# An inverse DFT in even and odd frequencies, q sums at full width, and cheaper tables in an attention-and-gate kernel

## The chip, the cores and the metric

The kernel runs on one core of a Trainium2 chip. The metric is the device time of one execution in microseconds. Most executions agree within about 1%. Each run has a state: "slow" if it lies over 1.5% above the fastest of the same kernel.

A core has a matmul engine (TensorE, "PE" in the profile), an elementwise engine (VectorE, "DVE"), an engine for copies and activations (ScalarE, "ACT"), GpSimd ("POOL"), a queue for transfers (SyncE, "SP"), and 16 DMA engines that move the data.

## The reference, cut to what matters

Two stages run one after the other, for 8 batches of 576 positions.

```python
def _attn_ref(q, k, v):                      # (8, 8, 576, 64) each
    m = 32
    q_lm = q.reshape(B, H, m, S // m, D).mean(axis=3)      # landmarks: sums of 18 rows
    k_lm = k.reshape(B, H, m, S // m, D).mean(axis=3)
    A, Bm, C = sm(q, k_lm), sm(q_lm, k_lm), sm(q_lm, k)    # three softmaxes
    Z = ...                                                # pseudo-inverse of Bm
    for _ in range(6):
        Z = 2 * Z - Z @ Bm @ Z                             # Newton steps
    return A @ Z @ C @ v

def _moe_ref(x, w_proj, filter_fft, w_out):  # x: the attention's output, (8, 576, 512)
    x1, x2, x3 = split(x @ w_proj)
    X2 = np.fft.rfft(x2, n=S, axis=1)
    H = np.fft.rfft(filter_fft, n=S, axis=0)
    y = x1 * np.fft.irfft(X2 * H, n=S, axis=1) * x3        # S = 576
    return y @ w_out
```

## The kernel before: the parts that the argument touches

The program is a prologue (load, landmarks and attention of batch 0, sine and cosine tables, spectrum of the filter) and then eight "gates". Gate `b` is woven step by step with the attention of batch `b + 1`, so that TensorE has work of one while the other waits.

The q sums add rows in groups of 18 with matmuls against a 0/1 matrix. A matmul takes a pair of a head's six columns. The middle pair belongs half to landmarks 0 to 15 and half to landmarks 16 to 31, so it is done as two matmuls that write 64 output rows each:

```python
def pool_q(h0):
    pl2 = st["pl"].rearrange("p (t h l) -> p t h l", t=2, h=H)
    for h in range(h0, h0 + 4):
        for x in (0, 2):
            mm(pl2[:, 1, h, :], qn[:, h, 2 * x:2 * x + 2, :]..., poolq[:, x // 2, :],
               start=(x == 0), stop=False)
        for par in range(2):
            mm(pl2[64 * par:64 * par + 64, 1, h, :], qn[:, h, 2 + par, :],
               poolq[:, par, :], start=False, stop=True)
```

The inverse DFT makes both halves of the 576 positions (`e` = 0, 1) from all frequencies, and VectorE multiplies the result in PSUM with the gates:

```python
def inverse(j):
    pi = wtile()
    for f in range(2):
        for t in range(2):
            for e in range(2):
                mm(pi[:, e, 0:HS], st["Y"][:, f, t, P * j:P * j + P],
                   INV[:, 2 * f + t, HS * e:HS * e + HS], ...)
    o = slice(64 * (j // 2), 64 * (j // 2) + 64)
    for e in range(2):
        mm(pi[:, e, 0:HS], st["YE"][o, ...], INV[o, 4, HS * e:HS * e + HS], ...)
    nc.vector.tensor_tensor(st["y"][:, j, :]..., pi[:, :, 0:HS], st.pop(f"gt{j}"), op=ALU.mult)
```

The filter is prepared in these lines. The tag of a tile names the ring of (here two) buffers that it is taken from; the tables' scratch tile `u` also has the tag "Y":

```python
def trig(dst, t, np_, shape):
    u = big.tile([np_] + shape, F32, tag="Y", name="u")
    ...                                     # three VectorE instructions and one Sin per table part
def filter_spectrum():
    fs = big.tile([R, 2, 3, Dm], F16, tag="Y", name="fs")
    nc.vector.tensor_tensor(fs[:, 0], filt[:, 0], filt[:, 1], op=ALU.add)
    nc.vector.tensor_tensor(fs[:, 1], filt[:, 0], filt[:, 1], op=ALU.subtract)
    ...
```

At the end of each gate `output(n)` multiplies the `y` of all four `j` with `wout`.

The softmax here doesn't subtract the row's maximum and nothing guards it: scores larger than these inputs give would overflow.

## Time and profile before

| | before |
|---|---|
| median of 3 runs | 293.62 us (293.33 to 296.63) |
| span of the profiled run, granted clock | 291.9 us, 0.972 |
| first AE matmul of the eight gates (first forward transform) | 52.7, 84.6, 114.2, ... 263.9 us |
| first spectral product on VectorE (`T`) of the eight gates | 61.1, 92.4, 122.0, ... 269.2 us |
| period of an undisturbed gate | 29.56 us |
| of it: first `T` to last `y`, last `y` to next `T` | 18.2 and 11.4 us |

The last four rows are read from the timeline; two of the seven periods were about 1 us longer at a lower granted clock.

The page of the kernel before: busy time by engine with its share of the span, then busy tenths of TensorE and VectorE in 40 slices of 7.3 us.

```profile
PE 249.2 (85%) x3642; PEld 149.3 (51%) x3642; DVE 166.6 (57%) x365; ACT 145.9 (50%) x247; POOL 31.9 (11%) x69
PE   0776108979999999999999999999989998999990
DVE  1279994066834684368417761867186718682830
```

After the prologue (the first seven slices) TensorE is full, and nothing else is. The 85% is an average of a prologue with holes and a steady state with hardly any. A window in the steady state shows that; columns: window, its length, then busy time and instructions of PE, weight loads, DVE, ACT and POOL, granted clock, DMA share, GB/s.

```profile
220.00:250.00 30.00, 29.20 (x467) 17.74 (x465) 17.53 (x36) 17.09 (x30) 0.00 (x0) 1.00 0.15 41
```

TensorE is busy for 29.20 of 30 us. The chain of waits through one period (92.4 to 122 us), shares by engine and line, agrees: 79% of it is matmuls.

```profile
by line: PE w L77 55.5%; PE s L77 23.7%; DVE T L580 8.3%; ACT X L578 3.5%; ACT G L569 3.1%; ACT eC L301 2.0%; DVE Y L582 2.0%; ACT lmp L211 2.0%; PE s L393 1.7%; DVE Bn L235 0.8%; issue 0.7%; DVE rB L232 0.4%; DVE rB L233 0.3%
```

The groups that the change touches; columns: line, engine, operation, out<-in, count, then busy us and mean ns of one, then the idle time of the engine just before them and what ended it.

```profile
L77 PE MATMUL w<-INV,Y 128*128 128x288 f16 x256 | 37.7, 287 | 0.2 <-ACT x_5153 L614 0.2
L631 DVE TENSOR_TENSOR y<-w,gt 128x576 bf16<-128x576 f32 x32 | 24.1, 752 | 11.0 <-PE w L77 11.0
L77 PE MATMUL w<-wout,y 128*128 128x512 bf16 x128 | 30.2, 380 | 0.0
```

The 287 ns are the time from a matmul's start to its modelled end. What a matmul costs in a full queue is the distance to the next start, and that is read from TensorE's timeline (start, duration of the group, what):

```profile
205.45 0.45 PE L77 MATMUL s<-poolk,kn 96*128 96x32 bf16 x12
...
206.97 1.20 PE L77 MATMUL s<-poolq,qn 96*128 96x32 bf16 x16
...
226.52 1.16 PE L77 MATMUL w<-INV,Y 128*128 128x288 f16 x8
227.61 0.41 PE L77 MATMUL w<-INV,YE 64*128 64x288 f16 x2
227.95 0.20 PE L77 MATMUL s<-RZ,identh 128*128 128x64 f16 x1
```

One inverse goes from 226.52 to 227.95: 1.43 us. Sixteen q sums take 1.13 us to the next start where twelve k sums of the same size take about 0.3: the q sums alternate between 128 and 64 output rows.

The prologue in TensorE's timeline; the bracket is the idle time before the group and what ended it.

```profile
45.09 6.59 PE L77 MATMUL w<-fs,F 96*128 96x512 f16 x18 [14.54 <-DVE fs L501]
...
52.69 0.90 PE L77 MATMUL w<-F,AE 96*128 96x288 f16 x6
```

VectorE's timeline just before that, in the same columns:

```profile
43.72 0.45 DVE L408 TENSOR_TENSOR u<-u,t 128x288 f32<-128x288 f32 x1
44.08 0.95 DVE L501 TENSOR_TENSOR fs<-filt 96x1536 f16<-96x1536 bf16 x1
```

TensorE waits 14.54 us for the filter sums `fs`, and `fs` runs only when the last table's `u` is done.

### The profile page before, as it was taken

To read this page: it belongs to the slowest core of one execution; us is meant where nothing else is said; L and a number is where in the kernel's file an instruction comes from. 1 tells how busy PE (TensorE), PEld (TensorE's weight loads), DVE (VectorE), ACT (ScalarE), POOL (GpSimd) and SP (SyncE) were. 2 spreads that over 40 slices of the span, in tenths; PEclk is the share of its full clock that TensorE was granted. 3 is DMA by queue.
4 is the path that set the end of the run, shared out by engine and by line. 5 is a ranking of instruction groups with operands and counts; after the bars stand their busy time and mean duration, and the time that the engine had idled before them with its cause. 6 is when DMAs were issued, how large, how long until landed. Compare 5 with 4: busy or idle time off the path is not lost.

```text
span 291.9 us, 8299 instructions
## 1 busy us (share of the span) xinstructions
PE 249.2 (85%) x3642; PEld 149.3 (51%) x3642; DVE 166.6 (57%) x365; ACT 145.9 (50%) x247; POOL 31.9 (11%) x69
## 2 busy tenths in 40 slices
PE   0776108979999999999999999999989998999990
PEld 0653102636655565556555656565656565654550
DVE  1279994066834684368417761867186718682830
ACT  1036132776258724872467435852685169518421
POOL 8871000200111010101020102001000000000000
PEclk9999999978999999999979998999999999999998
DMA  7999999996689958995899489939500050005005
GB/s 93 201 209 199 198 178 180 175 158 83 91 165 183 135 90 147 191 147 86 147 183 141 77 138 188 153 59 142 164 3 2 2 162 2 2 2 163 2 0 162
DMA packets 66420, 35.07 MB, mean 120 GB/s; under 512 B 46736, under 2 KB 62096, under 8 KB 66384
## 3 DMA queue, kind: packets, MB, share of 16 engines
q0 software_dynamic: 27280, 16.84, 42.5%
q1 hardware_dynamic: 39104, 17.70, 29.8%
q8 instruction: 28, 0.46, 0.6%
q14 instruction: 8, 0.07, 0.1%
HBM read 33.69 MB, written 9.44 MB: 148 GB/s over the span
## 4 chain that ended last, share of the span: by engine, by line
PE 73%; DVE 11%; ACT 9%; DMA 3%; issue 2%; POOL 0%; ACTq 0%; POOLq 0%
PE w L77 50%; PE s L77 20%; DMA qn<-in_q_dram 3%; DVE T L580 3%; ACT X L578 2%; ACT eC L301 2%; ACT G L569 2%; PE s L190 1%; DVE Y L582 1%; PE s L393 1%; DVE u L408 1%; ACT lmp L211 1%; DVE u L405 1%; DVE t L439 1%; DVE Bn L235 1%
## 5 line engine op out<-in xcount | busy, mean ns | idle before, releaser
L77 PE MATMUL w<-AT,G 128*128 128x288 f16 x256 | 43.4, 292 | 0.8 <-ACT x_5179 L614 0.2
L77 PE MATMUL w<-INV,Y 128*128 128x288 f16 x256 | 37.7, 287 | 0.2 <-ACT x_5153 L614 0.2
L631 DVE TENSOR_TENSOR y<-w,gt 128x576 bf16<-128x576 f32 x32 | 24.1, 752 | 11.0 <-PE w L77 11.0
L77 PE MATMUL w<-wout,y 128*128 128x512 bf16 x128 | 30.2, 380 | 0.0
L77 PEld LDWEIGHTS <-G 128*128 128x128 bf16 x256 | 21.5, 99 | 13.9 <-issue 7.6
L215 DVE TENSOR_SCALAR lm<-s 128x512 bf16<-128x512 f32 x8 | 5.5, 690 | 38.8 <-PE s L77 38.8
L77 PEld LDWEIGHTS <-Y 128*128 128x128 bf16 x256 | 22.0, 98 | 8.5 <-DVE Y L582 1.4
L580 DVE TENSOR_TENSOR T<-X,HH 128x2048 bf16<-128x2048 bf16 x16 | 19.5, 1221 | 11.3 <-ACT X L578 11.3
L569 ACT CAST G<-w 128x1024 bf16<-128x1024 f32 x24 | 24.4, 1016 | 0.2
L644 ACT COPY os<-w 128x1024 f32<-128x1024 f32 x16 | 16.2, 1013 | 15.8 <-PE w L77 15.8
L77 PE MATMUL w<-G,Ah 128*128 128x512 bf16 x64 | 20.7, 427 | 3.0 <-ACT eC L301 2.9
L77 PEld LDWEIGHTS <-y 128*128 128x128 bf16 (+1 forms) x192 | 14.2, 101 | 15.1 <-issue 2.3
L301 ACT ACTIVATE eA<-w 96x512 bf16<-96x512 f32 x24 | 14.1, 596 | 13.4 <-PE w L77 13.4
L77 PE MATMUL s<-poolq,qn 96*128 96x32 bf16 (+1 forms) x256 | 19.6, 196 | 0.9 <-DMA qn<-in_q_dram 0.9
L377 ACT CAST ZC<-s 128x256 bf16<-128x256 f32 x8 | 3.0, 373 | 33.8 <-PE s L77 33.8
L77 PE MATMUL w<-fs,F 96*128 96x512 f16 x18 | 6.6, 548 | 14.5 <-DVE fs L501 14.5
L77 PEld LDWEIGHTS <-qn 96*128 96x128 bf16 (+1 forms) x256 | 15.1, 104 | 6.8 <-issue 1.6
L397 DVE COPY AT<-s 128x576 f16<-128x576 f16 x16 | 7.2, 456 | 19.2 <-PE s L393 19.2
L578 ACT CAST X<-w 128x1024 bf16<-128x1024 f32 x16 | 16.4, 1022 | 3.6 <-PE w L77 3.5
L287 ACT CAST RZ<-s 128x128 f16<-128x128 f32 x40 | 10.6, 265 | 12.7 <-PE s L77 12.7
L556 ACT CAST Ah<-w 128x576 f16<-128x576 f32 x16 | 10.2, 640 | 13.4 <-PE w L77 13.3
L77 PE MATMUL w<-F,AE 96*128 96x288 f16 x96 | 16.6, 287 | 0.0
(232 smaller groups left out, 417.1 us busy)
## 6 DMA issues: line engine op xcount, KB each, us to landing
kn<-in_k_dram POOLq DMA_DIRECT2D x8, 576.0 KB, 8.5
qn<-in_q_dram POOLq DMA_DIRECT2D x8, 576.0 KB, 8.5
out_dram<-os SPq DMA_DIRECT2D x24, 192.0 KB, 2.5
vb_73<-in_v_dram POOLq DMA_DIRECT2D x4, 576.0 KB, 8.8
vb_76<-in_v_dram POOLq DMA_DIRECT2D x4, 576.0 KB, 7.5
out_dram<-os SPq DMA_DIRECT2D x16, 128.0 KB, 2.4
wproj<-in_moe_w_proj_dram POOLq DMA_DIRECT2D x3, 512.0 KB, 16.5
out_dram<-os SPq DMA_DIRECT2D x24, 64.0 KB, 2.0
```

Of the source, the lines that this page charges most:

```text
L77: nc.tensor.matmul(out_, lhsT, rhs, start=start, stop=stop, skip_group_check=True)
L215: nc.vector.tensor_scalar(lm.rearrange("p t h l -> p (t h l)"), pl3, 1.0 / blk, None, op0=ALU.mult)
L287: nc.scalar.copy(nx, pn)
L301: nc.scalar.activation(e[:, 2 * x:2 * x + 2, :], pc[:R, :, 0:256], AF.Exp, bias=0.0, scale=scale)
L377: nc.scalar.copy(ZC.rearrange("p g x -> p (g x)"), pz[:, 0:256])
L397: nc.vector.tensor_copy(res["AT"][:, g, :], pt[:, :S])
L556: nc.scalar.copy(st["Ah"][:, g].rearrange("p t (e r) -> p t e r", e=2), pf[:, :, 0:HS].rearrange("p e (t r) -> p t e r", t=2))
L569: nc.scalar.copy(st["G"][:, :, Dm * jb:Dm * (jb + 1)], pg)
L578: nc.scalar.copy(X, px)
L580: nc.vector.tensor_tensor(T, X.unsqueeze(2).to_broadcast([P, 2, 2, Dm]), HH[:, f], op=ALU.mult)
L631: nc.vector.tensor_tensor(st["y"][:, j, :].rearrange("p (e s) -> p e s", e=2), pi[:, :, 0:HS], st.pop(f"gt{j}"), op=ALU.mult)
L644: nc.scalar.copy(os, po)
```

## The change

It has four parts.

1. Inverse: positions n and n + 288 get the even frequencies with the same sign and the odd ones with opposite signs. So the even and the odd frequencies are transformed once each for one half (four matmuls instead of eight, plus two of 32 rows), and ScalarE and VectorE join them: `uo` is a copy of the odd half, then sum and difference, then the product with the gates. The copy is needed because a VectorE instruction takes at most one tensor input from PSUM (the Trainium skill, "PSUM — Partial Sum Buffer", Specifications (TRN2)).
2. q sums: three full-width matmuls per head, 16 columns each; the middle one goes to its own region, and two more matmuls fold it in.
3. Tables: sine and cosine from shared angles, computed before the first attention.
4. Newton's identity part as eight 32x32 matmuls instead of one of 128x128.

```diff
@@ q sums and landmarks
-                for x in (0, 2):
-                    mm(pl2[:, 1, h, :], ..., poolq[:, x // 2, :], start=(x == 0), stop=False)
-                for par in range(2):
-                    mm(pl2[64 * par:64 * par + 64, 1, h, :], qn[:, h, 2 + par, :],
-                       poolq[:, par, :], start=False, stop=True)
+                for x in range(3):
+                    lhsT = qn[:, h, 2 * x:2 * x + 2, :].rearrange("p c d -> p (c d)")
+                    if x == 1:
+                        mm(pl3[:, h, :], lhsT, poolq)
+                    else:
+                        lo = 8 * x
+                        mm(pl2[:, h, lo:lo + 16], lhsT, poolq[:, lo:lo + 16])
...
-            lmp = sm.tile([P, 512], F16, tag="lmp", name="lmp")
+            lmp = sm.tile([P, 768], F16, tag="lmp", name="lmp")
...
+            for par in range(2):
+                l = slice(16 * par, 16 * par + 16)
+                mm(o3[:, :, l], dup01[:, par, :], i3[:, :, l], start=False)
@@ newton
-            mm(pn[:, 1], identh, RZ[:, 1], start=True, stop=False)
...
+                for a in range(4):
+                    o = slice(32 * a, 32 * a + 32)
+                    mm(pn[o, 1, g, :], i32[o], RZ[o, 1, g, :], start=True, stop=False)
@@ tables (cut)
-    def trig(dst, t, np_, shape):
-        u = big.tile([np_] + shape, F32, tag="Y", name="u")
...
+        t = big.tile([R, 3, n], F32, tag="T", name="t")
...
+        w = big.tile([R, 3, n], F32, tag="T", name="w")
...
+    tables_fwd(kc, nrow)
+    tables_inv(sc, kb)
     res = {0: {}}
     a0 = attention(0, res[0], first=True)
...
-    tables_fwd()
-    tables_inv()
     filter_spectrum()
@@ inverse
             for f in range(2):
                 for t in range(2):
-                    for e in range(2):
-                        mm(pi[:, e, 0:HS], st["Y"][:, f, t, P * j:P * j + P],
-                           INV[:, 2 * f + t, HS * e:HS * e + HS], ...)
+                    mm(pi[:, f, 0:HS], st["Y"][:, f, t, P * j:P * j + P],
+                       INV[:, 2 * f + t, :], start=(t == 0), stop=False)
+            for f in range(2):
+                o = slice(64 * (j // 2) + 32 * f, 64 * (j // 2) + 32 * f + 32)
+                mm(pi[:, f, 0:HS], st["YE"][o, ...], INV[o, 4, :], start=False, stop=True)
+            cv_ = big.tile([P, 2, HS], BF16, tag="cv", name="cv", bufs=3)
+            uo = big.tile([P, HS], F32, tag="uo", name="uo")
+            nc.scalar.copy(uo, pi[:, 1, 0:HS])
+            nc.vector.tensor_tensor(cv_[:, 0, :], pi[:, 0, 0:HS], uo, op=ALU.add)
+            nc.vector.tensor_tensor(cv_[:, 1, :], pi[:, 0, 0:HS], uo, op=ALU.subtract)
             nc.vector.tensor_tensor(st["y"][:, j, :]...,
-                pi[:, :, 0:HS], st.pop(f"gt{j}"), op=ALU.mult)
+                cv_, st.pop(f"gt{j}"), op=ALU.mult)
```

## The prediction

> **What bounds the kernel now.** Span 291.9 us, in three parts. (1) A prologue: the first gate's forward transform (AE matmuls) starts at 52.7 us. The timeline shows VectorE almost solid from 22 to 45 us with the sine and cosine tables, TensorE idle 14.5 us waiting for the filter sums, then 18 filter matmuls at 0.42 us. (2) Seven batches of 29.56 us, TensorE 97% busy (windows 100-250). (3) A last gate of 28 us.
>
> **Removed.**
> - Inverse: per j, eight 288-column matmuls of 0.124 us (start to start) become four; the two YE matmuls move to different row groups and may overlap. A j takes 1.43 us of TensorE; I estimate 0.80: 2.5 us per batch.
> - q sums: their matmuls start 67-70 ns apart, the like k sums' 27 ns. The Trainium skill ("TensorEngine Tiling (Array Packing)", Key Properties) says that changing the tiling mode drains TensorE; the trace agrees: only the q sums alternate 128- and 64-column outputs. 2.26 us becomes about 0.75: 1.5 us per batch.
> - Tables: about 19 us of VectorE work becomes about 9, put ahead of the first attention, in VectorE's early idle time (8 of its first 10 us, half of the next 10).
>
> **Added, per batch.**
> - VectorE: one 752 ns product with a PSUM input becomes two of 288 columns with fp32 inputs plus one bf16 product. The skill ("VectorE: DVE Perf Modes", TRN2 errata and perf-mode tier table) gives (N+151)/0.96 ns for an fp32 tensor_tensor and doubles 16-bit SBUF ones; the trace agrees (576 columns 752 ns; 256 bf16 columns 289 ns). So 3 x 0.45, less overlaps: +0.45 us each, +1.8 per batch.
> - ScalarE: four fp32 copies of 288 columns, about 0.40 us each (256 take 0.377), and a wider landmark copy: +1.6 us, net of overlaps.
> - TensorE: 16 more forward columns (0.08), two landmark matmuls (0.1), Newton's eight small ones for one large (about 0).
>
> **The critical path.** TensorE saves 3.8 us per batch, but I do not expect to see it all. From the first spectral product to the last y (18.2 us of the period) VectorE idles only 2.6 us; it gets 1.8 us more there while TensorE gets 2.5 less. That stretch becomes VectorE-bound and hardly shrinks. From the last y to the next spectral product (11.4 us) the q sums save 1.5, but ScalarE's copies (os, os, osr, Ah, G, Ah, lmp, G, X, about 8.5 us) limit it, and the landmark sums now hold one of the three two-bank PSUM buffers. So the period falls by about 1.9 us, to 27.7. The prologue falls most: about 15 us, first gate near 38 us. Last gate -1, first gate -1.5.
>
> Sum: 38 + 30 + 6 x 27.7 + 27 + 1.7 (time over span) = **263 us**, range **254 to 273** (8 in 10). Faster by over 2%: 0.97; within: 0.02; slower: 0.01.
>
> **Signs.** Right: first AE matmul at 35-41 us; period 27-28.4; TensorE about 93% or less of it, VectorE about 70% with no idle gaps between X and the last y; q-sum step 0.4 us; INV,Y matmuls 128; joins near 0.45 us. Wrong on the bottleneck: TensorE still 97%, period near 25.8 (then about 250 us). Wrong on the prologue: extra activation-table loads or late AE put the first gate past 42.
>
> **What would make it wrong.** Sine/exp table switches delaying the first attention; input DMA (190 GB/s to 50 us) starving the second batch; PSUM buffers stalling TensorE (period 29); VectorE work slipping into its 5 us idle stretch, letting the whole TensorE saving through.

## The result, and the profile after

The changed kernel took 274.2 us (273.12 to 275.75, 4 runs), against 293.59 for the kernel before in the same rounds. The ratio is 0.9321 (95% interval 0.9241 to 0.9402). Here and below a ratio sets the fast runs of one kernel against those of the other in the same rounds, so it is not quite the ratio of the medians that stand beside it; those medians count slow runs too, and where there is one the text says so. The runs come from different rounds and chips, so two experiments are best compared by their ratios, with the intervals, and by their profiles. It is faster by 7%, but slower than the predicted 263 and just outside the range of 254 to 273.

Where the span went, from the timelines of the two profiled runs (spans 291.9 and 273.3 us):

| stretch | before | after | change | predicted after |
|---|---|---|---|---|
| start to first AE matmul | 52.7 | 46.8 | -5.9 | 38 |
| first AE to second AE (first gate) | 31.9 | 34.6 | +2.7 | 30 |
| second AE to last AE (six periods) | 179.3 | 164.3 | -15.0 | 166.2 |
| last AE to end | 28.0 | 27.5 | -0.5 | 27 |

Some 2 us of the third row's change belong to the lower granted clock in two periods of the kernel before. Counted by the first product `T` instead of AE, the prologue ends at 57.9 us against 61.1, and the first gate takes 29.7 against 31.3. So the period was predicted well (27.4 on average against 27.7), and what is missing lies before the second gate: its AE starts at 81.5 us, where the prediction's sum has 68.

The page after, the same three lines:

```profile
PE 218.4 (80%) x3773; PEld 126.6 (46%) x3796; DVE 172.4 (63%) x417; ACT 159.2 (58%) x288; POOL 28.9 (11%) x60
PE   0401569989898998899889988998899889989980
DVE  1029766358673788398837882978378829783950
```

VectorE's second slice, 2 before, is now 0. The same window as before, in the same columns:

```profile
220.00:250.00 30.00, 26.70 (x465) 15.04 (x461) 19.42 (x44) 21.12 (x37) 0.00 (x0) 1.00 0.19 52
```

The chain of waits through one period (142 to 170 us; the profile cuts the line off at its end):

```profile
by line: PE w L77 27.4%; issue 9.8%; DVE T L604 9.6%; PE s L77 7.9%; DVE gt L641 7.4%; ACT X L602 6.6%; DVE cv L660 5.3%; DVE cv L659 5.2%; ACT Ah L582 4.8%; DVE Y L606 4.3%; DVE y L662 4.2%; ACT G L593 3.3%; ACT lmp L220 2.5%; PE s L409 1.
```

TensorE is busy 89% of the window instead of 97%, and matmuls are 35% of the chain instead of 79%. This looks as if the bottleneck had moved to VectorE and ScalarE. Keep that reading in mind; the experiments do not bear it out.

The groups after:

```profile
L77 PE MATMUL w<-wout,y 128*128 128x512 bf16 x120 | 31.3, 381 | 4.8 <-DVE cv L660 4.1
...
L658 ACT COPY uo<-w 128x288 f32<-128x288 f32 x32 | 12.8, 399 | 24.1 <-PE w L77 17.6
...
L77 PE MATMUL w<-INV,Y 128*128 128x288 f16 x128 | 22.8, 289 | 0.4 <-ACT x_5443 L639 0.2
...
L659 DVE TENSOR_TENSOR cv<-w,uo 128x288 bf16<-128x288 f32 x32 | 14.4, 451 | 6.4 <-ACT uo L658 6.4
...
L662 DVE TENSOR_TENSOR y<-cv,gt 128x576 bf16<-128x576 bf16 x32 | 14.2, 444 | 0.2
```

Each predicted duration holds: half the INV,Y matmuls, the copy at 399 ns (0.40 predicted), the joins at 451 ns (0.45). What is new is in the first line: the output matmuls, which waited for nothing before, now wait 4.1 us in all for the last join `cv`. TensorE's timeline shows one place:

```profile
137.84 0.46 PE L77 MATMUL w<-poolq,qn 96*128 96x16 bf16 x12
...
155.50 0.66 PE L77 MATMUL w<-INV,Y 128*128 128x288 f16 x4
156.09 0.29 PE L77 MATMUL w<-INV,YE 32*128 32x288 f16 x2
156.32 0.20 PE L77 MATMUL s<-RZ,i_120 32*32 32x32 f16 x4
...
157.44 0.38 PE L77 MATMUL w<-wout,y 128*128 128x512 bf16 x1
158.44 0.60 PE L77 MATMUL w<-wout,y 128*128 128x512 bf16 x2 [0.62 <-DVE cv L660]
```

An inverse goes from 155.50 to 156.32, 0.82 us instead of 1.43 (0.80 predicted). The two YE matmuls take 0.29 us together, as long as one alone takes: they run side by side. That agrees with the Trainium skill ("TensorE: Matmul & The Clock Gate", Part 3), which has matmuls on different row groups start within about 4 ns of each other. Twelve q sums take 0.37 us to the next start, instead of 1.13 for sixteen.

Then the prologue. VectorE's timeline from the start:

```profile
1.78 0.06 DVE L508 MEMSET wk<- 1x1 f32 x1
18.93 0.95 DVE L528 TENSOR_TENSOR fs<-filt 96x1536 f16<-96x1536 bf16 x1 [17.09 <-DMA filt<-in_moe_filter_fft_dram]
19.81 0.95 DVE L529 TENSOR_TENSOR fs<-filt 96x1536 f16<-96x1536 bf16 x1
...
20.78 0.64 DVE L471 TENSOR_SCALAR t<-kc,nrow 96x289 f32<-96x289 f32 x2
```

The chain of waits of the first 40 us (start, duration, what):

```profile
4.74 14.17 DMA filt<-in_moe_filter_fft_dram
18.93 0.95 DVE fs L528
```

The first AE matmuls in TensorE's timeline:

```profile
46.83 1.68 PE L77 MATMUL w<-F,AE 96*128 96x304 f16 x6
```

VectorE stands still from 1.8 to 18.9 us. The two filter sums are now at the front of its queue, ahead of the tables and of the copies of the transposed k, and they wait for the filter's transfer. ScalarE and VectorE queues are strict first-in first-out (the Trainium skill, "PSUM — Partial Sum Buffer", Engine vs sequencer instructions, and the table at the top of "TensorE: Matmul & The Clock Gate"), and this trace agrees: 17.09 us in which nothing behind `fs` started. Nobody moved `fs` in the source. In the kernel before its buffer was held by `u` until 44 us; the change took `u` out of that ring, the buffer was free from the start, and the scheduler put `fs` where its only other condition is a transfer.

### The profile page after: what moved, and what is told of

The parts are those of the page before. It is cut to its first block, busy times and chain, and to the rows that moved or that the text cites. A ratio compares the mean times of both kernels' runs of the same rounds, so it can differ in the third digit from the quotient of the medians.

```text
span 273.3 us, 8670 instructions
## 1 busy us (share of the span) xinstructions
PE 218.4 (80%) x3773; PEld 126.6 (46%) x3796; DVE 172.4 (63%) x417; ACT 159.2 (58%) x288; POOL 28.9 (11%) x60
## 3 DMA queue, kind: packets, MB, share of 16 engines
q1 hardware_dynamic: 39104, 17.70, 32.2%
## 4 chain that ended last, share of the span: by engine, by line
PE 44%; DVE 27%; ACT 14%; issue 6%; DMA 5%; POOL 1%; ACTq 0%; DVEq 0%; POOLq 0%
PE w L77 33%; PE s L77 9%; DMA filt<-in_moe_filter_fft_dram 5%; DVE gt L641 4%; DVE T L604 3%; DVE cv L659 3%; DVE cv L660 3%; DVE y L662 2%; ACT Ah L582 2%; ACT G L593 2%; ACT X L602 2%; DVE Y L606 2%; PE s L409 2%; ACT lmp L220 2%; ACT eC L317 1%
## 5 line engine op out<-in xcount | busy, mean ns | idle before, releaser
L77 PE MATMUL w<-wout,y 128*128 128x512 bf16 x120 | 31.3, 381 | 4.8 <-DVE cv L660 4.1
L658 ACT COPY uo<-w 128x288 f32<-128x288 f32 x32 | 12.8, 399 | 24.1 <-PE w L77 17.6
L77 PE MATMUL w<-INV,Y 128*128 128x288 f16 x128 | 22.8, 289 | 0.4 <-ACT x_5443 L639 0.2
L199 PE MATMUL s<-ident,kn 96*128 96x96 bf16 x24 | 2.4, 276 | 22.6 <-DVE kT_74 L203 14.7
L77 PE MATMUL w<-G,Ah 128*128 128x512 bf16 x49 | 16.8, 393 | 2.6 <-ACT Ah L582 0.6
L659 DVE TENSOR_TENSOR cv<-w,uo 128x288 bf16<-128x288 f32 x32 | 14.4, 451 | 6.4 <-ACT uo L658 6.4
L77 PE MATMUL w<-F,AE 96*128 96x304 f16 x96 | 17.7, 313 | 0.3
L582 ACT CAST Ah<-w 128x608 f16<-128x608 f32 x16 | 10.7, 666 | 8.6 <-PE w L77 7.9
L317 ACT ACTIVATE eC<-w 96x512 bf16<-96x512 f32 x24 | 14.1, 597 | 1.5 <-PE w L77 1.3
L77 PE MATMUL s<-RZ,i_120 32*32 32x32 f16 x384 | 13.0, 182 | 1.9 <-issue 1.3
L662 DVE TENSOR_TENSOR y<-cv,gt 128x576 bf16<-128x576 bf16 x32 | 14.2, 444 | 0.2
```

The lines of the kernel that those rows point to most:

```text
L77: nc.tensor.matmul(out_, lhsT, rhs, start=start, stop=stop, skip_group_check=True)
L317: nc.scalar.activation(e[:, 2 * x:2 * x + 2, :], pc[:R, :, 0:256], AF.Exp, bias=0.0, scale=scale)
L582: nc.scalar.copy(st["Ah"][:, g], pf[:, :, 0:FW])
L658: nc.scalar.copy(uo, pi[:, 1, 0:HS])
L659: nc.vector.tensor_tensor(cv_[:, 0, :], pi[:, 0, 0:HS], uo, op=ALU.add)
L662: nc.vector.tensor_tensor(st["y"][:, j, :].rearrange("p (e s) -> p e s", e=2), cv_, st.pop(f"gt{j}"), op=ALU.mult)
```

## The experiments

The theories when the runs began. For the prologue: (A) the queue order behind `fs` costs about 10 us, all of which comes back if `fs` is moved; the rival: the input transfers, or loads of activation tables, bound the prologue, and moving `fs` gains less than 2 us. For the steady state: the prediction's theory, that the stretch from `T` to the last `y` is bound by VectorE, so that TensorE's savings there are lost; the rival: TensorE's time still counts in full, and the join gives a fixed part back. All runs were correct unless it is said. "Before" in each is the kernel before on the same chip.

### The filter sums back behind the tables (fs_late)

```diff
-        fs = big.tile([R, 2, 3, Dm], F16, tag="Y", name="fs")
+        fs = big.tile([R, 2, 3, Dm], F16, tag="T", name="fs")
```

The ring "T" is the one that the table tiles now use, so `fs` waits for them. Only the two additions move in VectorE's queue; the queues of all other engines are the same.

> The changed kernel with one edit: the tile of the filter sums (fs) takes a buffer that the forward tables hold first, so that its two additions stand behind the tables in VectorE's queue; every other queue is unchanged. Theory A (VectorE, which works its queue in order, stood 17 us behind the two additions that wait for the filter's DMA): VectorE's tables start near 9.5 us instead of 20.7, the first spectral product (T) starts near 48 us instead of 57.9, the time falls by 8 to 10 us to about 265 us, and the period of a batch stays at 27.4 us. Rival (the prologue is bound by input DMA at about 200 GB/s or by activation-table loads): T still starts at 56 us or later and the time stays within 2 us.

Measured: 268.81 us (before 295.18; ratio 0.9099, 0.9042 to 0.9155). The first AE comes at 36.6 us, 10.2 earlier, the first `T` at 47.4, 10.5 earlier. VectorE's timeline has the first table work at 10 us and `fs` behind it:

```profile
9.99 0.78 DVE L471 TENSOR_SCALAR t<-kc,nrow 96x289 f32<-96x289 f32 x2 [1.07 <-POOL nrow L429]
...
21.88 0.95 DVE L528 TENSOR_TENSOR fs<-filt 96x1536 f16<-96x1536 bf16 x1
```

But the first gate, `T` to `T`, grows from 29.7 to 34.7 us. TensorE's timeline of this run:

```profile
36.60 1.68 PE L77 MATMUL w<-F,AE 96*128 96x304 f16 x6
...
51.44 1.16 PE L77 MATMUL w<-AT,G 128*128 128x288 f16 x8 [0.17 <-ACT x L639]
57.35 0.21 PE L77 MATMUL w<-lm,qT 64*128 64x32 bf16 x2 [4.75 <-DMA qT<-qn]
```

The chain of waits of its first 85 us (start, duration, what):

```profile
11.13 16.43 DMA kn<-in_k_dram
27.57 6.24 SPq L102
33.86 23.44 DMA qT<-qn
```

What follows: the queue order is the cause of the late first gate, 10 us of it. But half of what is won is lost at once. TensorE waits 4.75 us for the transposed q of the second batch, which lands at 57.3 us, and in this run the granted clock after that wait was low: 0.50 between 60 and 65 us (the lowest in any 5 us of the changed kernel's first gate is 0.66). So not all of the 5 us is the wait itself; fs_join16 below, with a wait of 3.85 us and a clock of 0.94 in the same 5 us, has a first gate of 32.1. The prologue has two bounds, one behind the other. The period stays 27.4.

### The filter fetched earlier (filt_early)

```diff
+        if b == 0:
+            load_filter()          # between the transfers of q and v
...
-        if jb == 1:
-            filt = ...; nc.gpsimd.dma_start(filt..., moe_filter_fft...)
```

> The changed kernel with the filter's DMA issued third (before v and the projection weights) instead of fifth; the additions stay first in VectorE's queue. Theory A: the filter lands near 13 to 14 us instead of 18.9, VectorE's long wait shrinks from 17 to about 12 us, and T starts about 5 us earlier (53 us); time about 269 us. Rival (DMA or table loads bind): less than 2 us gained.

Measured: 270.51 us (median of four, one of them slow; before 295.18; ratio 0.912, 0.9035 to 0.9205). The profiled run is the slow one; in it the first `T` is at 52.5 us and the first gate takes 32.2. What follows: shortening the wait instead of moving it gives part of the same gain, so it is the wait for the filter that costs, not the two additions.

### The inverse of before in the changed kernel (old_inverse)

```diff
-                    mm(pi[:, f, 0:HS], st["Y"]..., INV[:, 2 * f + t, :], ...)
+                    for e in range(2):
+                        mm(pi[:, e, 0:HS], st["Y"]..., INV[:, 2 * f + t, HS * e:HS * e + HS], ...)
...
-            (uo, the two joins, y = cv_ * gt)
+            y = pi[:, :, 0:HS] * gt
```

> The changed kernel with the inverse as it was before: both halves by TensorE (eight and two matmuls a step), one VectorE product straight from PSUM, no ScalarE copy; the second halves of the tables are made from the first by five small VectorE operations (about 1.5 us once). Theory B (from the first spectral product to the last y VectorE is the limit, so the split moved work from TensorE to VectorE with nothing left over): that stretch stays at 18.0 to 18.6 us, the period at 27.4 to 28, time 274 to 279 us. Rival (TensorE still limits that stretch): the period rises by 2.5 us to 29.9, time near 292 us.

Measured: 283.16 us (before 295.18; ratio 0.9606, 0.9525 to 0.9686). The period is 28.60 us, 18.23 from `T` to the last `y` and 10.37 from there to the next `T`. That is more than the 274 to 279 us expected with VectorE as the limit, and less than the 292 of the rival. (The edit also makes the second halves of the tables with some small VectorE operations in the prologue; the first `T` stays at 57.9 us.) The split is worth 1.2 us per batch (28.60 to 27.40), nearly all of it seen after the last `y` and not in the stretch that holds the inverse.

### The q sums of before in the changed kernel (old_q)

The edit puts `poolq`, the two sums and the landmark step of before back.

> The changed kernel with the q landmark sums and the landmark step as before (128- and 64-column matmuls in turn, one single-bank PSUM buffer). Theory B: the steady gain came from the stretch between the last y and the next spectral product, so it goes from 9.4 back to about 11 us, the period from 27.4 to about 29, time about 285 us. Rival (the three two-bank buffers were what held that stretch, and the new sums, which take one of them, gained little): the time rises by less than 4 us.

Measured: 288.45 us (median of four, one of them slow; before 295.18; ratio 0.9755, 0.9683 to 0.9827). The period is 29.08 where it is undisturbed and the first `T` is at 60.7 us instead of 57.9; the first AE, at 46.5 us, does not move. So the q sums are worth 1.7 us per batch and 2.8 us between the first AE and the first `T`, more than the 1.5 per batch that TensorE's time alone was predicted to save.

### The join taken out (no_join; wrong result, relative error 0.707)

```diff
-            (cv_, uo, copy, add, subtract)
             nc.vector.tensor_tensor(st["y"][:, j, :]...,
-                cv_, st.pop(f"gt{j}"), op=ALU.mult)
+                pi[:, :, 0:HS], st.pop(f"gt{j}"), op=ALU.mult)
```

> Wrong result on purpose: the changed kernel with its halved inverse, but without the join: y is the two half sums times the gate in one VectorE product, as before, and no ScalarE copy. It is the new TensorE work with the old VectorE and ScalarE work. Theory B (VectorE limits the stretch from the first spectral product to the last y): the stretch falls from 18.0 to 15.7 to 16.5 us, the period from 27.4 to 25.3 to 26, time 260 to 264 us. Rival (something else than VectorE's load limits it): the period stays above 27.

Measured: 266.4 us (before 294.93; ratio 0.9049, 0.9005 to 0.9093), period 26.60. Removing about 1.8 us of VectorE's busy time and 1.4 of ScalarE's per batch makes the period 0.8 us shorter. The `T` to last `y` stretch falls to 16.35 us, but the rest grows to 10.25.

### The inverse's large matmuls done twice (twice_inverse)

```diff
-            for f in range(2):
+            for f in (0, 1, 0, 1):
                 for t in range(2):
                     mm(pi[:, f, 0:HS], st["Y"]..., INV[:, 2 * f + t, :], start=(t == 0), ...)
```

The second pass starts the sum afresh, so the result is right, and TensorE has 16 more matmuls of 0.124 us per batch, 2.0 us. VectorE's and ScalarE's work is the same. If the stretch is bound by VectorE, this costs little.

> The changed kernel with its four product matmuls of a step issued twice (the second set starts the sums over; the result is right): TensorE has the old inverse's 2.0 us more per batch, VectorE and ScalarE keep the join. Theory B (VectorE is the limit, with TensorE close behind it): the period rises by 0.3 to 1.3 us, less than the 2.0 us added. Rival (TensorE is the limit): the whole 2.0 us, period 29.4, time near 288 us.

Measured: 288.71 us (before 294.93; ratio 0.9781, 0.975 to 0.9812). The first `T` of two gates in turn, in VectorE's timeline of this run:

```profile
147.13 1.23 DVE L604 TENSOR_TENSOR T<-X,HH 128x2048 bf16<-128x2048 bf16 x1 [0.59 <-ACT X L602]
...
176.59 1.23 DVE L604 TENSOR_TENSOR T<-X,HH 128x2048 bf16<-128x2048 bf16 x1 [0.60 <-ACT X L602]
```

The period is 29.46: 2.06 us more for 2.0 us of matmuls. TensorE's time counts in full. The prediction's theory of a stretch bound by VectorE falls.

The four kernels form a table of periods:

| | no join | join |
|---|---|---|
| long inverse | 28.60 (old_inverse) | 29.46 (twice_inverse) |
| short inverse | 26.60 (no_join) | 27.40 (after) |

TensorE's 2 us are worth 2.00 and 2.06 us, the join costs 0.80 and 0.86. The two add; neither hides the other. (The two long inverses are not quite the same: in old_inverse the YE matmuls also go one after the other.)

TensorE's own account of one undisturbed period shows the same. From one first `T` to the next, in us, with the idle time as period less busy time:

| | period | TensorE busy | TensorE idle |
|---|---|---|---|
| before | 29.56 | 28.75 | 0.81 |
| after (two periods in turn) | 27.53, 27.25 | 24.98, 25.07 | 2.55, 2.18 |
| no_join | 26.60 | 24.74 | 1.86 |
| old_inverse | 28.60 | 26.70 | 1.90 |
| twice_inverse | 29.46 | 27.05 | 2.41 |
| short_sum (below) | 27.55 | 25.16 | 2.39 |
| old_q_inverse (below) | 29.96 | 28.35 | 1.61 |

TensorE's busy time fell by 3.7 us per batch, the 3.8 that the prediction saved. What was lost is 1.6 us of new idle time. Two more us of matmuls leave the idle time as it was, and so does 1.2 us less of VectorE. The join accounts for about 0.5 us of it; the rest is there without the join too.

The group of output matmuls tells where the join's part sits. In the run without the join:

```profile
L77 PE MATMUL w<-wout,y 128*128 128x512 bf16 x120 | 28.6, 380 | 1.2 <-issue 1.1
```

With the join (shown above) the same group has 31.3 us busy and 4.8 us idle before it: 2.7 and 3.6 us more over eight batches, together 0.79 us per batch. That is the size of the join's cost. At the outputs one matmul goes ahead, and what ends TensorE's wait there is the last join: it reads the PSUM buffer that the next output needs.

### A faster join from a 16-bit copy (fs_join16)

```diff
 (fs_late, and)
+            ho = big.tile([P, 2, HS], F16, tag="uo", name="uo", bufs=3)
+            nc.scalar.copy(ho, pi[:, :, 0:HS])
-            (uo, and joins from pi[:, 0] and uo)
+            nc.vector.tensor_tensor(cv_[:, 0, :], ho[:, 0, :], ho[:, 1, :], op=ALU.add)
+            (and the same with subtract)
```

> The late filter sums together with a cheaper join: ScalarE copies both half sums from PSUM to a 16-bit tile (576 columns, about 0.64 us instead of 0.40), and VectorE adds and subtracts 16-bit data (about 0.31 us each instead of 0.45). VectorE loses about 1.1 us per batch, ScalarE gains about 0.9, and the PSUM buffer is free after the copy. Theory B: the stretch from the spectral product to the last y shrinks by 0.5 to 1 us against the late filter sums alone, the period to 26.4 to 26.9, time 4 to 7 us below that run. Rival (VectorE is not the limit): no gain, or a loss from ScalarE.

Measured: 267.54 us (before 294.93; ratio 0.9064, 0.9039 to 0.909). The period is 27.36 against 27.38 and the stretch 18.10, so nothing is gained per batch. Its small lead over fs_late is in the first gate, 32.1 us instead of 34.7, and there the granted clock differed (0.94 against 0.50 between 60 and 65 us), so it need not be the join's. Moving the join's work from VectorE to ScalarE doesn't help. The wait for `cv` at the outputs is gone (1.1 us before the output group in all, 5.4 in fs_late), but TensorE now waits 0.70 us per period for `Zb`, which comes from the Newton steps and whose matmuls stand just ahead: the wait has moved.

### Both old parts back (old_q_inverse)

The edits of old_q and old_inverse together; what is left of the change are the tables and Newton's matmuls.

> The changed kernel with both the old inverse and the old q sums: what is left of the change is the tables and Newton's small matmuls. Theory B: the period goes back to 29.3 to 29.9 us (29.56 before), and the time to 287 to 291 us; the rest of the gap to the kernel before (3 to 6 us) is the prologue. Rival (the tables' new place costs nothing and gains the 15 us predicted): 280 us or less.

Measured: 296.86 us (before 294.93; ratio 1.0063, 1.0035 to 1.0091), period 29.96 where it is undisturbed, first `T` at 60.6 us against 61.1 of the kernel before. So the tables, as the change placed them, gained 0.5 us. The period is 0.4 us longer than before. The table above shows where: TensorE is busy 0.4 us less and idle 0.8 more. In the kernel before, three output matmuls stand in TensorE's queue ahead of those that read `Zb`, and these don't wait; here only one does, and TensorE waits 0.33 us for `Zb` and 0.16 after it. So the order of TensorE's queue changed too; which part of the change moved it was not tested. The periods form a ladder: 29.96, with the new q sums 28.60, with the split too 27.40. By the other way, over old_q, it is 29.96, 29.08, 27.40: the parts do not quite add, and the q sums are worth 1.4 or 1.7 us and the split 0.9 or 1.2, by what else is there.

### The third batch's loads held back (fs_hold)

```diff
 (fs_late, and in load)
+        if b == 2:
+            nc.gpsimd.tensor_copy(kn[:, 0, 0, 0:2], qTbufs[1][0:R, 0, 0:2])
+            nc.gpsimd.tensor_copy(qn[:, 0, 0, 0:2], qTbufs[1][0:R, 0, 0:2])
```

Two columns of the second batch's transposed q are copied into the third batch's buffers, so that the third batch's loads wait for those transposes and don't compete with them. The loads overwrite the columns.

> The late filter sums, and the loads of k and q of the third batch held until the q transposes of the second batch have landed (a tiny copy from the transposed tile into the load's target). Theory C (with the filter wait gone, the second bound of the prologue is the second batch's transposed q: it came at 57.3 us with the late filter sums, because the third batch's loads, issued at 20 us instead of 30, shared the DMA engines with it): q lands at 46 to 50 us, TensorE's wait of 4.75 us for it goes, the first gate's T-to-T distance falls from 34.7 to about 30 us, time 263 to 265 us (268.8 without the hold). Rival (the transposes are slow for another reason): the wait stays, 268 us or more.

Measured: two fast runs, 266.25 and 269.02 us, and two slow ones (275.0 and 276.58; before 295.45; ratio of fast runs 0.9042, 0.8949 to 0.9135). The profiled run is a slow one, so its times are only a guide to the order of events; the fast run of fs_first_hold below shows the same order. SyncE's timeline of the q transposes of the second and third batch:

```profile
33.88 5.35 SPq L105 DMA_TRANSPOSE qT<-qn  x1
...
57.51 10.88 SPq L105 DMA_TRANSPOSE qT<-qn  x1
```

The second batch's wait is gone (first gate 28.1 us), and the second and third gate pay for it with 35.6 and 32.1 us. Holding back only moves the wait. The limit may be the volume of bytes needed in the first 60 us (151 to 208 GB/s in each 10 us of fs_late from 10 us on); no run isolates it, and the hold itself leaves the transfers thin: 113 GB/s between 40 and 50 us in fs_first_hold, against 151 in fs_late. The Trainium skill ("Trainium Kernel Development and Optimization", Key Constraints) says that DMAs from the SP and POOL queues run on the same 16 engines and interleave. The changed kernel's trace agrees: the issue of a q transpose took 12.12 us beside the loads of the third batch's k and q, and 2.97 us where no load was in flight. It need not be the third batch's loads: in fs_first_hold, which holds them back, it took 12.22 us beside the second batch's v and the output weights. SyncE's timeline of the changed kernel:

```profile
34.14 12.12 SPq L102 DMA_TRANSPOSE qT_78<-qn  x1
...
69.23 2.97 SPq L102 DMA_TRANSPOSE qT_78<-qn  x1
```

### The second batch's k and q ahead of two weight parts (fs_first)

```diff
 (fs_late, and)
+    def load_kq(b): (the k and q transfers of load, issued earlier)
...
     nc.gpsimd.dma_start(filt..., moe_filter_fft...)
+    load_kq(1)                     # then the projection weights' other two parts
```

> The late filter sums, and the second batch's k and q loads issued before the second and third part of the projection weights (6 us instead of 11), without the hold. Theory C: k lands near 21 to 23 us instead of 27.5, the transposes start 5 us earlier and are done before 50 us, time 263 to 266 us. Rival (the DMA engines carry the same bytes, so something else comes late, such as the weights): 268 us or more.

Measured: 266.03 us (265.13 to 268.52; before 295.45; ratio 0.9001, 0.8933 to 0.907). The first `T` is at 49.8 us, 2.4 later than in fs_late, the first gate takes 30.4 us instead of 34.7 (part of which is again the granted clock: 0.80 against 0.50 between 60 and 65 us), and TensorE's first matmul with that q waits 0.22 us, for ScalarE, and not for the transfer. It has the lowest median of the correct kernels, but its interval overlaps those of fs_late, fs_hold and fs_join16, so their order is not settled.

### Both (fs_first_hold)

> Both: second batch's k and q first, third batch's held. Theory C: the transposes are done by 42 us, no TensorE wait for them; time 262 to 264 us, the lowest of the study. Rival: the third batch comes late now and the second gate grows by what the first one lost; 267 us or more.

Measured: 270.49 us (median of four, one of them slow; before 295.45; ratio 0.9107, 0.9027 to 0.9187); first `T` at 49.5, gates of 28.6, 31.9 and 28.7 us. The hold takes more from the second gate than it gives to the first. Its copy was made an addition with columns of the forward table, so that it sits behind the table in GpSimd's queue.

### Newton's identity as before (old_newton)

```diff
+            mm(pn[:, 1], identh, RZ[:, 1], start=True, stop=False)
...
-                for a in range(4):
-                    mm(pn[o, 1, g, :], i32[o], RZ[o, 1, g, :], start=True, stop=False)
```

> The changed kernel with Newton's step as before (one 128-row matmul with the identity in place of eight 32-row ones). From the trace a step's TensorE time is 0.22 us now and 0.30 before, six steps per batch. If TensorE time counts in full, the period rises by 0.4 to 0.5 us and the time by 3 to 4 us, to about 277.5; if the step is only part of a chain through ScalarE, by less than 1 us in all; if the small matmuls cost more than they save, as the 0.4 us per batch that the kernel with old inverse and old q sums is slower than the kernel before suggests, it falls by 2 to 3 us.

Measured: 273.64 us (before 295.45; ratio 0.9256, 0.9193 to 0.9319), period 27.41, first `T` at 58.2. This part of the change is worth nothing that shows, as predicted ("about 0"), though the step itself starts its successor after 0.22 instead of 0.30 us.

### Less of another VectorE work (short_sum; wrong result, relative error 62.9)

```diff
-                rA, eA.rearrange("p c (h l) -> p (c h) l", l=m), axis=AX.X,
+                rA, eA.rearrange("p c (h l) -> p (c h) l", l=m)[:, :, 0:8], axis=AX.X,
```

The row sums of the softmax read a quarter of their input: 540 ns instead of 1740 in VectorE, 1.2 us less per batch, and nothing else.

> Wrong result on purpose: the changed kernel with the row sums of the first softmax taken over 8 of 32 columns (VectorE's reduction of 1.74 us becomes about 0.55); nothing else. Theory B (VectorE's load limits the stretch from the first spectral product to the last y): the stretch falls from 18.0 to about 16.8 to 17.2 us, the period from 27.4 to 26.2 to 26.6, time near 266 to 268 us. Rival (a chain that passes through all three engines, or TensorE's own time, limits it): the period falls by less than 0.4 us, time above 271 us.

Measured: 274.52 us (before 295.01; ratio 0.9295, 0.9258 to 0.9331), period 27.55 instead of 27.40. VectorE's load is not the limit. The stretch from `T` to the last `y` even grew, from 18.0 to 18.44 us, since the freed VectorE ran other work before the last product; its timeline in this run:

```profile
156.41 0.94 DVE L379 TENSOR_TENSOR A<-eA,rA 96x1536 f16<-96x1536 bf16 x1
...
159.44 0.54 DVE L400 TENSOR_TENSOR AE<-A 96x768 f16<-96x768 f16 x1
159.91 0.45 DVE L662 TENSOR_TENSOR y<-cv,gt 128x576 bf16<-128x576 bf16 x1
```

And the same place in VectorE's timeline of the changed kernel:

```profile
160.09 0.39 DVE L662 TENSOR_TENSOR y<-cv,gt 128x576 bf16<-128x576 bf16 x1
...
160.63 0.95 DVE L379 TENSOR_TENSOR A<-eA,rA_3298 96x1536 f16<-96x1536 bf16 x1
```

So "the stretch between two events" was not a fixed piece of work, and the prediction should not have been argued from it. The period is the measure.

### The same sums by folding, with a right result (fs_first_fold)

```diff
 (fs_first, and)
+            nc.vector.tensor_tensor(hA, e4[:, :, 0:m // 2], e4[:, :, m // 2:m], op=ALU.add)
+            nc.vector.tensor_tensor(qA, hA[:, :, 0:m // 4], hA[:, :, m // 4:m // 2], op=ALU.add)
+            nc.vector.tensor_reduce(rA, qA, axis=AX.X, op=ALU.add)
-            (one reduce over 32)
```

> The late filter sums and the second batch's k and q first (266.0 us), with the same row sums made by two 16-bit half-length additions and a reduction of a quarter of the length: about 1.3 us in place of 1.74, right result. Theory B: the period falls by 0.3 to 0.5 us, time 263 to 264 us. Rival: no change within 1 us.

Measured: 269.92 us (before 295.01; ratio 0.9145, 0.9101 to 0.919), period 27.85. It is slower than fs_first. The three instructions that replace a sum of 1740 ns take 546, 345 and 549 ns, so only 0.3 us could be had. Why the folded sums lengthen the period by 0.45 us was not looked into.

## Why the prediction was right or wrong, point by point

- **"The prologue falls most: about 15 us, first gate near 38 us."** This is the step that failed. The first AE came at 46.8 us, and the second gate's AE at 81.5 us instead of 68, 13.5 us late. The cost of the tables and the idle time that they were to fill were read rightly, but the order of VectorE's queue was assumed to stay. The removal of `u` freed the buffer of `fs`, and the scheduler put `fs`, which waits for a transfer, in front: VectorE stood still for 17.09 us. fs_late shows the assumed place: AE at 36.6 us, within the predicted 35 to 41.
- **"First gate -1.5", 30 us.** It took 34.6 us from AE to AE. Counted by `T` it was 29.7. In fs_late, with the prologue as assumed, it is 34.7 by `T` and 39.3 from AE to AE, because of the q transposes and, in that run, a low granted clock after them: "input DMA ... starving the second batch" was named as a risk, and was given no time. So even with the right queue order the kernel takes 268.8 us and not 263. With the loads reordered too (fs_first) it takes 266.0.
- **"So the period falls by about 1.9 us, to 27.7."** Right in size: 29.56 to 27.40 on average, and 27.25 and 27.53 in turn.
- **"That stretch becomes VectorE-bound and hardly shrinks."** The stretch hardly shrank (18.2 to 18.0 us), but the reason was wrong. twice_inverse shows that TensorE's time counts in full (2.06 us for 2.0), short_sum that 1.2 us less of VectorE changes nothing, and no_join that the join costs 0.8 us. Two errors met: TensorE's busy time fell in full, by 3.7 us, and its idle time grew by 1.6 (0.81 to 2.4), nearly what the VectorE bound was thought to cost. That the period came out so near was luck.
- **Added times.** Copy 399 ns, joins 451 and 447 ns, product 444 ns: as predicted. The formula of the Trainium skill ("VectorE: DVE Perf Modes", TRN2 errata) for an fp32 add gives an estimate of (288 + 151)/0.96 = 457 ns for the join; the trace has 447 to 451.
- **q sums.** Predicted 2.26 to 0.75 us of TensorE per batch; measured from start to start 2.25 to 0.75 or 0.94 in turn, plus the two matmuls that fold the middle part in. They were worth 1.7 us in the period beside the new inverse, 1.4 beside the old one.
- **TensorE "about 93% or less", VectorE "about 70% with no idle gaps between X and the last y".** TensorE 89%, VectorE 65% in the window shown; VectorE was idle for 2.0 to 2.6 us there. The missing half of this sign was a hint against the VectorE bound.
- **Last gate.** 27.5 us against 27. Right.

What stays open: which part of the change reordered TensorE's queue and so made old_q_inverse 0.4 us per batch slower than the kernel before, and why TensorE's idle time of about 2.4 us stays nearly the same whether matmuls are added or VectorE's work is cut. The tables show this as a fact and not its cause; given that, the period follows TensorE's busy time one to one, though matmuls are only 35% of the chain of waits. A join that reads both halves from PSUM and row sums on GpSimd have no run.

## What to carry to other kernels

Before costing a change, look at which buffers it frees: in an engine with an in-order queue, an instruction that a buffer held back can move to the front and block everything behind it on a transfer, and the diff will not show it. After a wait is removed, look for the next one at the same place (here the filter's 17 us, then the transposed q's 4.75), and give each a time in the sum. To find out what bounds a steady state, don't read it off the chain of waits or from the idle time of a stretch; double the suspected work and cut the rival's, and see which one the period follows. Then split the period into the busy and the idle time of the engine that it follows: here the saving arrived in full and new idle time took part of it back.

## What the Trainium skill lacked or had wrong

- "TensorEngine Tiling (Array Packing)", Key Properties, says that a change of the tiling mode drains TensorE, but not what it costs. Here sixteen q sums that alternate between 128 and 64 output rows took 1.13 us from the first start to the next group's, against 0.30 us for twelve of one width; that is about 45 ns more for each matmul. No run took the alternation away alone.
- "TensorE: Matmul & The Clock Gate" and "PSUM — Partial Sum Buffer" state that VectorE's queue is first-in first-out, but neither warns that the order that a scheduler puts into it can change with a buffer that becomes free. It cost 17.09 us of standing still, and undoing it gained 5.4 us between the medians of different rounds (274.2 to 268.8), or about 6.5 us by the two ratios to the kernel before (0.9321 and 0.9099).
- No section that I found on transposing DMAs in "DMA: Bandwidth & Descriptors" says how much they slow down beside loads: in the changed kernel the issue of a transpose of q took 2.97 us with no load in flight and 12.12 us beside the loads of k and q.
- "VectorE: DVE Perf Modes", TRN2 errata, was right: an estimate of 457 ns by its formula, 447 to 451 measured. So was Part 3 of "TensorE: Matmul & The Clock Gate": two matmuls on different row groups took 0.29 us together.
